# Seven block products instead of eight in the first half of a feed-forward, and a regrouped attention loop

## The chip, the cores and the metric

The kernel runs on one core of a Trainium2 chip. The metric is the device time of one execution in microseconds (us). Three executions of the kernel before took 1903.85, 1904.07 and 1905.6 us; the median is 1904.07 us. A separate profiled execution took 1902.24 us, of which 1900.5 us lie between its first and its last instruction (the span). The five engines are TensorE (PE in the profile), VectorE (DVE), ScalarE (ACT), GpSimd (POOL) and SyncE (SP); each works through a queue of its own, in order. TensorE writes its results to PSUM, eight banks of 2 KB per partition; VectorE and ScalarE move them from there to SBUF, GpSimd works in SBUF alone.

## What is computed

One transformer block on 2048 tokens of width 576, in float32:

```python
sa, ca, ga, sb, cb, gb = split(silu(c) @ w_mod, 6)
h = layernorm(x) * (1 + ca) + sa
x = x + ga * attention(h)          # 32 heads of 18, 4 segments of 512, causal inside a segment,
                                   # blended with a linear-attention memory of earlier segments
h = layernorm(x) * (1 + cb) + sb
x = x + gb * ((silu(h @ w_gate) * (h @ w_up)) @ w_down)      # 4608 wide
```

To keep float32 accuracy with TensorE's faster float32r products, each operand is split in a high and a low part, and a product is done as three: high by high, high by low, low by high.

## The kernel before, in words

**Stages.** Projections and the first attention units take the span up to about 258 us, attention goes on to about 618 us, a hand-over stretch follows, and the feed-forward runs from about 645 us to the end. It handles the tokens in two halves of 1024 (`t` 0 and 1). For each half it walks over 18 pairs `p` of 128-wide column groups of the 4608.

**One pair.** A pair has 14 steps (`k`). Each step is one block product of a seven-product (Strassen-like) scheme for gate (`z` 0) and up (`z` 1): `prod` (L1200), seven matmuls of 512 columns into bank A, B or C. Into the same steps the down product of the pair before is placed, in chunks. There are two forms of it. `plain` (L1321) is the ordinary block product: 8 chunks of 12 matmuls of 288 columns, 96 in all, each chunk added to its accumulator by VectorE (L1325). `down` (L1304) is the seven-product form: 14 chunks of 6 matmuls, 84 in all, each added by VectorE (L1309); it needs four sums of activations (`sum_a`, L1271), seven split activations (`prep_a`, L1264 and L1265) and seven split weights (`prep_d`, L1189 and L1190) where `plain` needs four of each. The function `is_plain` says which: the whole first half and the last two pairs of the second half are plain. Where chunks stand is written by hand in `CH` and `CH0`.

**Weights.** In the first half each weight tile `O` (gate or up, one pair) is loaded from the input, GpSimd makes four sums of its slots (`sum_o`, L1155), ScalarE and VectorE split each slot (`prep_w`, L1164 and L1165), and the sums are stored for the second half. The 288 input rows are 256 plus 32; the 32 left-over rows lie in a third column block of `O` and are split by `prep_r` (L1149, L1150) into the tile `R`, which is stored for the second half too. The down weights are scaled by `gb` and summed by GpSimd (`mul_d` L1178, `sum_d` L1183). Meanwhile `prep2` makes the second half's input: layernorm, transposes on TensorE (L1102), splits (L1058, L1062), sums.

**Attention.** 32 units of 4 heads (four segments, eight units each). Per unit three generators run side by side in 11 slots: score products with a running maximum on VectorE (`p1_step`, L182 and L187), score products with an exponential on ScalarE and a causal mask on GpSimd (`p2_step`, L599, L602 and L606), and the products with v (`av_step`, L619: plain float32, a 32-column weight tile per head, four heads side by side). The strings in `PAT` place everything else by hand: `V0` to `V3` are the four v steps (0 and 1 of this unit, 2 and 3 of the unit before), in four places of the unit. PSUM: two banks for the maximum's scores, two for the exponential's, one for v, two shared ones (tag `x`), one for the output projection.

**Hand-over** (L1380 to L1450). The last output projection (`wo_m`, L729), whose results VectorE adds (`wo_x`, L734), is interleaved with the first weight sums, the first `prep_r` and the first `prep_w`.

Of the kernel before, what the change touches and what calls it, by code (L numbers as in the profile page):

```python
# [15 lines left out]
P = 128  # L16
S = 2048
# [20 lines left out]
CH0 = ((0, 0, 0, 0, 1, 1, 1, 1, 1, 1, 1, 1, 0, 0), (0, 0, 0, 1, 1, 1, 1, 1, 1, 1, 1, 0, 0, 0))  # L38
RS = {(0, 5): 2, (0, 6): 4, (0, 8): 3, (0, 10): 5, (1, 9): 2, (1, 11): 3, (1, 13): 4}
# [14 lines left out]
G2 = (2, 3, 4, 5, 6, 7, 8, 9, 10, 11)  # L54
# [5 lines left out]
PAT = (["", "V2", "V3 E m D", "M0", "n M1 Q G", "c", "M2 d", "V0 g", "h A0 q M3 R S X", "T Y Z B0", "A1 P V1 z B1 f C"],  # L60
# [3 lines left out]
LNA = 1  # L64
S1B, S2B, XB, WB = 2, 2, 2, 1
# [7 lines left out]
def block(ctx: ExitStack, tc: tile.TileContext, x, wqk, wv, wo, beta, wgu, wd, c, w_mod, out):  # L73
# [76 lines left out]
    rD = [[dr.tile([96, 7, P], F32, tag=f"rD{p}_{z}", name=f"rD{p}_{z}") for z in range(2)] for p in range(NF // 2)]  # L150
# [5 lines left out]
    mcol, pmt, mrow = {}, {}, {}  # L156

    def load_stack(u, b):
        s, q = units[u]
        for e in range(2):  # L160
            v = [d[s].rearrange("f z t -> (f z) t").rearrange("(Q a e r) t -> Q e r a t", Q=8, a=2, e=2)[q, e]
                 for d in (kD, qD)]
            r = slice(54 * e, 54 * e + 54)
            nc.sync.dma_start(f32(kst[b][r]), v[0])
            nc.sync.dma_start(f32(qst[b][r, e:4:2, :]), v[1])
# [6 lines left out]
    def p1_step(u, b, i, ps, jp, jb):  # L172
# [6 lines left out]
        for h0 in range(0, 4, per):  # L179
            bank = ps.tile([P, L], F32, tag="s1", name="s1", bufs=S1B)  # L180
# [407 lines left out]
    def p2_step(u, j):  # L588
# [4 lines left out]
        pt = pp_.tile([P, 4, n], F32, tag=f"P{j}", name="Pt", bufs=1)  # L593
        Pt[u, j] = pt
        for h in range(0, 4, per):
            bank = ps.tile([P, L], F32, tag="s2", name="s2", bufs=S2B)
            for g in range(h, h + per, 2):
                w = min(per, 2)
                nc.tensor.matmul(bank[:, n * (g - h):n * (g - h + w)].rearrange("p (a b) -> p a b", a=w),  # L599
                                 lhsT=kst[u % NB][0:110, g // 2, 128 * j:128 * j + 128],  # L600
                                 rhs=qst[u % NB][0:110, g:g + w, 128 * j:L], start=True, stop=True)
            nc.scalar.activation(pt[:, h:h + per, :n], bank[:, :n * per].rearrange("p (a b) -> p a b", a=per),  # L602
                                 AF.Exp, scale=SCALE)
            if h + per < 4:
                yield
# [4 lines left out]
    def av_step(u, j):  # L610
# [3 lines left out]
        if j == 0:  # L614
            av[u] = ps.tile([P, L], F32, tag="av", name="av", bufs=1)
# [227 lines left out]
    def event(ev, u):  # L843
        n, a = ev[0], ev[1:]
        s, q = divmod(u, 8)
        if n == "V":
            j = int(a)
            av_step(u if j < 2 else u - 1, j)
# [185 lines left out]

    def y_sum(kb):
# [13 lines left out]

    def prep2(x2p):  # L1050
# [4 lines left out]
        def opr(kb, hv, o, f):  # L1055
            n = P if kb < 2 else 96
            st = x2p.tile([P, 2, 256], F32R, tag="st", name="st", bufs=4)
# [28 lines left out]
        for kb in range(3):  # L1086
            n = P if kb < 2 else 96
            for hv in range(2):
                for kh in range(2):
# [10 lines left out]
                    pt = ps.tile([P, 2, L], F32, tag="dn", name="pt", bufs=2)[:, 0].rearrange("p (a b) -> p a b", b=P)  # L1100
# [31 lines left out]
    def load_o(t, p, z):  # L1132
        O[p, z] = o = opl.tile([P, 7, 3, P], F32, tag="O", name="O", bufs=2)
        if t == 0:
            nc.sync.dma_start(o[:, 0:4], wgu[p, z])
        else:
            nc.sync.dma_start(o[:, 0:3, 0:2], wgu[p, z][:, 0:3, 0:2])
            nc.sync.dma_start(o[:, 3:7, 0:2], oD[p][z])

    def store_o(p, z):  # L1140
        nc.scalar.dma_start(oD[p][z], O[p, z][:, 3:7, 0:2])

    def prep_r(t, p, z, part=0):
        r = R[z]
        if t == 1:
            (nc.sync if p or z == 0 else nc.scalar).dma_start(f32(r[0:96]), rD[p][z])
            return
        o, c = O[p, z], slice(0, 3) if part == 0 else slice(3, 7)
        nc.scalar.copy(r[0:96, c], o[0:96, c, 2, :])  # L1149
        later.append(lambda: nc.vector.tensor_tensor(r[32:64, c], o[32:64, c, 2, :], f32(r[32:64, c]), op=ALU.subtract))  # L1150

    def sum_o(p, z, j, eng=nc.gpsimd):
        o = O[p, z]
        d, a, b, op = ((4, 3, 2, ALU.add), (5, 4, 0, ALU.subtract), (3, 0, 3, ALU.subtract), (6, 1, 5, ALU.subtract))[j]
        eng.tensor_tensor(o[:, d], o[:, a], o[:, b], op=op)  # L1155

    def store_r(p, z):
        nc.scalar.dma_start(rD[p][z], f32(R[z][0:96]))

    def prep_w(p, z, m):  # L1160
        o = O[p, z][:, SLOT[m], 0:2]
# [14 lines left out]
    def mul_d(p, f):  # L1176
        v = RW[p][:, 2 * f:2 * f + 2].rearrange("p a b -> p (a b)")
        nc.gpsimd.tensor_tensor(v, v, gbB, op=ALU.mult)  # L1178

    def sum_d(p, j):  # L1180
        r = RW[p]
        d, a, b = ((4, 1, 0), (5, 3, 4), (6, 2, 5), (1, 3, 1))[j]
        nc.gpsimd.tensor_tensor(r[:, d], r[:, a], r[:, b], op=ALU.subtract)  # L1183
# [101 lines left out]

    def load_x11(t):
# [9 lines left out]
    def down(t, p, c):  # L1296
        m, c = POS[c // 2], c % 2
        ah, al = AP[p % 2, m]
        dh, dl = DP[p % 2, m]
        pd = ps.tile([P, 2, L], F32, tag="dn", name="pd", bufs=2)  # L1300
        for i in range(2):
            tk = slice(128 * (2 * c + i), 128 * (2 * c + i) + 128)
            for k, (a, w) in enumerate(((ah, dh), (ah, dl), (al, dh))):
                nc.tensor.matmul(pd[:, i, :288], lhsT=a[:, tk], rhs=w, start=(k == 0), stop=(k == 2))  # L1304
        o = acc[m][:, 2 * c:2 * c + 2]
# [5 lines left out]
    def plain(t, p, c):  # L1311
        b, h, c = c // 4, c // 2 % 2, c % 2
        pd = ps.tile([P, 2, L], F32, tag="dn", name="pd", bufs=2)
# [9 lines left out]
        d = x11[1] if t and b and h else acc[2 + h + 2 * b]  # L1323
# [8 lines left out]
    def comb(j):  # L1332
        d, b = ((2, 1), (0, 5), (6, 1), (5, 6), (3, 5), (7, 6), (4, 7), (0, 7))[j]
        d = acc[d] if d else x11[1]
# [5 lines left out]
    with tc.manual_schedule():  # L1340
        new_stack(3, sk2)
# [4 lines left out]
        for u in range(NU + 1):  # L1346
            s, q = divmod(u, 8)
            load_unit(u + 3)
            ga = chain(*[p2_step(u, j) for j in range(4)])
            gb = p1_seq(u + 2)  # L1350
            for k in range(11):
                next(ga, None)
                next(gb, None)
                if u == 17 and k == 0:
# [30 lines left out]
        load_o(0, 0, 1)  # L1385
        load_y(0, 1)
# [13 lines left out]
        for i in range(4):  # L1400
            for h in range(2):
                for c in range(WC):
# [12 lines left out]
                    if n in WW:  # L1415
                        j = WW.index(n)
                        if j < 2:
                            prep_r(0, 0, 0, j)
# [26 lines left out]
        for t in range(2):  # L1445
            for p in range(NPR):
                last = t == 1 and p == NPR - 1
# [3 lines left out]
                if t == 0 and p == 1:  # L1451
                    p7.close()
                    x2p = pool(p6, "x2p")
                    g2 = prep2(x2p)
                if t == 0 and p == NPR - 1:
                    run(g2)
                    p6.close()
                    accq = pool(p4, "acq")
                    new_acc(accq, (1, 6, 7))
                if last:  # L1460
                    load_x11(1)
                chunk = 0
                for k in range(14):
# [6 lines left out]
                    for f in todo:  # L1470
                        f()
                    while acts:
# [14 lines left out]
                    if t:  # L1487
                        if k == 2 + swap:
                            prep_r(1, p, 1)
                        elif not last and k == 9:  # L1490
                            prep_r(1, nx, 0)
                    else:
                        if k in (3, 5):
                            prep_r(0, p, 1, k // 5)
                        elif tn == 0 and k in (9, 10):
                            prep_r(0, nx, 0, k - 9)
# [138 lines left out]
```

## Time and profile before

| | us |
|---|---|
| median of three executions | 1904.07 |
| profiled execution | 1902.24 |
| its span | 1900.5 |
| TensorE busy in the span | 1862.9 |
| VectorE busy | 1509.0 |
| ScalarE busy | 933.8 |
| GpSimd busy | 584.4 |

A busy TensorE is counted from the start of a matmul to its modelled end, and matmuls overlap: a 288-column matmul is listed with about 0.29 us, but the next one starts 0.13 us later. The cost of a matmul in a dense stretch is therefore the distance between starts. In the rows of the timeline, the columns are the start, the length, the engine, the line, the operation with its output and inputs, the shape, the count, and in brackets the idle time before it with what ended it. In the grouped rows, the columns are the busy time in us, the mean length of one in ns, and the idle time ahead of the group.

### The profile page before, as it was taken

How to read it: one execution, taken by the hardware profiler on the slowest of the kernel's cores; microseconds unless marked ns; L12 is line 12 of the kernel's file. 1: busy time of each engine (PE TensorE's matmuls, PEld its weight loads, DVE VectorE, ACT ScalarE, POOL GpSimd, SP SyncE). 2: the span in 40 equal slices, each digit the busy share in tenths (PEclk: the TensorE clock that was granted, in tenths of full speed). 3: DMA queues.
4: the chain of work that ended last, by engine and by line, in shares of the span. 5: the costliest groups of instructions: out<-in, count | busy, mean ns of one | idle time of the engine just before them, and what ended most of it. 6: DMA issues, size and time to landing. Idle time of an engine off the chain costs nothing.

```text
span 1900.5 us, 30716 instructions
## 1 busy us (share of the span) xinstructions
PE 1862.9 (98%) x10927; PEld 1559.2 (82%) x10927; DVE 1509.0 (79%) x3277; ACT 933.8 (49%) x2060; POOL 584.4 (31%) x789
## 2 busy tenths in 40 slices
PE   6999999999999899999999999999999999999999
PEld 4888866676766788888888888888888888888888
DVE  6566358878886688898898888876888888888887
ACT  1222267768767444445454454444445454454542
POOL 5212236555556555545544545400000000000000
PEclk9999999999999899999999999999999999999999
DMA  6767555446654854454454454378343233333331
GB/s 190 259 221 249 200 193 155 132 136 175 184 159 127 282 201 160 157 196 158 153 189 158 164 171 149 135 262 257 102 123 104 85 115 102 124 102 101 108 108 59
DMA packets 179424, 304.31 MB, mean 160 GB/s; under 512 B 26152, under 2 KB 107688, under 8 KB 177352
## 3 DMA queue, kind: packets, MB, share of 16 engines
q1 hardware_dynamic: 150696, 245.29, 40.9%
q10 hardware_dynamic: 28576, 57.07, 8.6%
q8 instruction: 86, 1.41, 0.3%
q14 instruction: 66, 0.54, 0.1%
HBM read 187.98 MB, written 113.77 MB: 159 GB/s over the span
## 4 chain that ended last, share of the span: by engine, by line
PE 90%; DVE 3%; DMA 2%; ACT 2%; POOL 1%; issue 1%; SPq 0%; ACTq 0%; DVEq 0%; POOLq 0%
PE A L1200 23%; PE pd L1321 13%; PE C L1200 12%; PE pd L1304 9%; PE B L1200 6%; PE pp L99 6%; PE s L599 4%; PE av L619 4%; PE s L182 4%; PE pv L99 2%; PE pw L729 2%; PE pn L800 1%; PE px L640 1%; ACT Pt L602 1%; PE pm L448 1%
## 5 line engine op out<-in xcount | busy, mean ns | idle before, releaser
L1200 PE MATMUL A<-y,wh 128*128 128x512 f32 x1152 | 404.5, 392 | 1.7 <-ACT B L1246 1.1
L187 DVE CUSTOM_DVE_ANT_0 junk<-s,tri 128x256 bf16<-128x256 f32 (+3 forms) x512 | 228.4, 486 | 68.4 <-PE s L182 60.9
L1165 DVE TENSOR_TENSOR wl<-O,wh 128x256 fp32r<-128x256 f32 x504 | 264.1, 529 | 3.3 <-ACT wh L1164 2.8
L1200 PEld LDWEIGHTS A<-y,wh 128*128 128x128 f32 x1152 | 216.7, 188 | 42.6 <-ACT B L1246 1.7
L1200 PE MATMUL A<-y,wl 128*128 128x512 f32 x576 | 224.8, 390 | 0.0
L602 ACT ACTIVATE Pt<-s 128x512 f32<-128x512 f32 (+1 forms) x352 | 187.9, 559 | 70.2 <-PE s L599 64.4
L1155 POOL TENSOR_TENSOR O<-O 128x384 f32<-128x384 f32 x140 | 158.1, 1142 | 174.3 <-DMA O<-in_wgu_dram 78.8
L1200 PE MATMUL C<-y,wh 128*128 128x512 f32 x576 | 203.6, 394 | 3.8 <-DMA y<-yD 2.5
L1309 DVE TENSOR_TENSOR acc<-acc,pd 128x576 f32<-128x576 f32 x216 | 162.2, 751 | 54.8 <-PE pd L1304 50.6
L1164 ACT CAST wh<-O 128x256 fp32r<-128x256 f32 x504 | 196.9, 405 | 0.8 <-issue 0.7
L1321 PE MATMUL pd<-dh,ah 128*128 128x288 f32 x640 | 189.8, 297 | 0.3 <-DVE acc L1325 0.3
L1321 PE MATMUL pd<-dh,al 128*128 128x288 f32 x640 | 188.2, 294 | 0.0
L1321 PE MATMUL pd<-dl,ah 128*128 128x288 f32 x640 | 188.1, 294 | 0.0
L1325 DVE TENSOR_TENSOR acc<-acc,pd 128x576 f32<-128x576 f32 x156 | 116.7, 749 | 81.8 <-PE pd L1321 81.7
L1264 ACT CAST ah<-sg 128x512 fp32r<-128x512 f32 x192 | 119.3, 621 | 86.1 <-DVE sg L1224 80.4
L599 PE MATMUL s<-qs,ks 110*128 110x512 f32 (+2 forms) x384 | 150.1, 407 | 2.9 <-ACT Pt L602 2.4
L182 PE MATMUL s<-ks,qs 108*128 108x256 f32 (+3 forms) x512 | 140.4, 327 | 1.9 <-DVE mx L187 1.8
L1265 DVE TENSOR_TENSOR al<-sg,ah 128x512 fp32r<-128x512 f32 x192 | 135.6, 707 | 7.1 <-ACT ah L1264 6.8
L1304 PE MATMUL pd<-dh,ah 128*128 128x288 f32 x448 | 132.9, 297 | 0.0
L1304 PE MATMUL pd<-dl,ah 128*128 128x288 f32 x448 | 131.9, 294 | 0.0
L1304 PE MATMUL pd<-dh,al 128*128 128x288 f32 x448 | 131.2, 293 | 0.0
L1200 PEld LDWEIGHTS C<-y,wh 128*128 128x128 f32 x576 | 108.1, 188 | 24.1 <-DMA y<-yD 2.9
(364 smaller groups left out, 4410.9 us busy)
## 6 DMA issues: line engine op xcount, KB each, us to landing
O<-in_wgu_dram SPq DMA_DIRECT2D x36, 768.0 KB
oD<-O ACTq DMA_DIRECT2D x36, 512.0 KB
O<-oD SPq DMA_DIRECT2D x36, 512.0 KB
ks<-kD SPq DMA_DIRECT2D x64, 216.0 KB
qs<-qD SPq DMA_DIRECT2D x64, 216.0 KB
O<-in_wgu_dram SPq DMA_DIRECT2D x36, 384.0 KB
rD<-wr ACTq DMA_DIRECT2D x36, 336.0 KB
wr<-rD SPq DMA_DIRECT2D x35, 336.0 KB
```

Of the source, the lines that this page charges most:

```text
L99: nc.tensor.matmul(ps, lhsT=a, rhs=b, start=(k == 0), stop=(k == 13))
L182: nc.tensor.matmul(bank[:, n * (h - h0):n * (h - h0) + n], lhsT=qst[b][0:108, h, 128 * i:128 * i + 128], rhs=kst[b][0:108, h // 2, 0:n], s ...
L187: nc.vector.tensor_tensor_reduce(junk[:, :n], bank[:, n * (h - h0):n * (h - h0) + n], tri[:, L - n:], 1.0, -3e38, op0=ALU.add, op1=ALU.max ...
L599: nc.tensor.matmul(bank[:, n * (g - h):n * (g - h + w)].rearrange("p (a b) -> p a b", a=w), lhsT=kst[u % NB][0:110, g // 2, 128 * j:128 * ...
L602: nc.scalar.activation(pt[:, h:h + per, :n], bank[:, :n * per].rearrange("p (a b) -> p a b", a=per), AF.Exp, scale=SCALE)
L1155: eng.tensor_tensor(o[:, d], o[:, a], o[:, b], op=op)
L1164: nc.scalar.copy(wh, o)
L1165: later.append(lambda: nc.vector.tensor_tensor(wl, o, f32(wh), op=ALU.subtract))
L1200: nc.tensor.matmul(bank, lhsT=a, rhs=b, start=(first and n == 0), stop=(n == 6), skip_group_check=not first)
L1304: nc.tensor.matmul(pd[:, i, :288], lhsT=a[:, tk], rhs=w, start=(k == 0), stop=(k == 2))
L1309: nc.vector.tensor_tensor(o, o, pd[:, :, :288], op=ALU.add)
L1321: nc.tensor.matmul(pd[:, i, :288], lhsT=a[:, tk], rhs=w, start=(k == 0), stop=(k == 5))
```

## The change

In the first half, pairs 0 to 15 now use the seven-product form of the down product, as the second half does; only the last two pairs of each half stay plain. The first half's accumulators are combined in its last pair (`comb`, eight additions), as was done in the second half alone.

- **Chunks on ScalarE.** In the first half, for pairs 1 to 15, the odd chunks (seven of fourteen) do not go through VectorE: ScalarE first copies the accumulator into the PSUM bank (`preload`), TensorE adds the products to it, and ScalarE copies the sum back. The two PSUM buffers of the down product become two tags of one buffer each, `dn0` for even and `dn1` for odd chunks.
- **Left-over rows.** `prep_r` is gone. The left-over rows are an input of their own (`wgr`), summed by GpSimd, copied by ScalarE and subtracted by GpSimd in the attention stage (`stage_r`: nine batches, one every two units, 4 sums, 4 copies and 4 subtractions each), stored, and loaded into `R` by three DMAs per weight tile in both halves. `O` shrinks from three column blocks to two.
- **GpSimd in pieces.** `sum_o` works in pieces of 128 elements per partition, eight per weight tile where there were four of 384; `mul_d` and `sum_d` in pieces of 144 (before 576 and 288). `mul_d` and `sum_d` move to steps 3 to 5, the first tile's `sum_o` to steps 5 to 8.
- **Second half's preparation.** `prep2` may go on in 13 steps of a pair instead of 10; its transposes use `dn0` in steps 6, 7 and 12 alone, and it has three split buffers instead of four.
- **Attention.** The four v steps of a unit are done in one burst at the start of the next unit, between the first score product and its exponential, and their bank comes from the shared tag `x`. The maximum's scores get a third bank. The stacked q and k are loaded in pieces of 96 and 12 and of 48 and 6 partitions instead of 54, as an event of the pattern. `PAT` is rewritten.

```diff
-S1B, S2B, XB, WB = 2, 2, 2, 1
+S1B, S2B, XB, WB = 3, 2, 2, 1
...
+    def stage_r():
...
+            for j, (d, x_, y_, op) in enumerate(SUMS):
+                at(max(0, g + RL[1 + j]), lambda ...: nc.gpsimd.tensor_tensor(o[:, d], o[:, x_], o[:, y_], op=op))
+            for j in range(4):
+                c = slice(32 * j, 32 * j + 32)
+                at(g + RL[5 + j], lambda ...: nc.scalar.copy(h[:, :, c], o[:, :, c]))
+                at(g + RL[9 + j], lambda ...: nc.gpsimd.tensor_tensor(o[:, :, c], o[:, :, c], f32(h[:, :, c]), op=ALU.subtract))
...
+    def preload(t, p, c):
+        if t == 0 and p > 0 and c in AS:
+            PRE[c] = pd = new_dn("pd", c)
+            nc.scalar.copy(pd[:, :, :288], chunk_of(c))
...
     def down(t, p, c):
+        o = chunk_of(c)
+        pd = PRE.pop(c, None)
+        add = pd is None
+        if add:
+            pd = new_dn("pd", c)
...
+        if not add:
+            outs.append(lambda: nc.scalar.copy(o, pd[:, :, :288]))
+            return
...
     def is_plain(t, p):
-        return t == 0 or p >= NPR - 2
+        return p >= NPR - 2
...
             for k in range(11):
                 next(ga, None)
+                if k == BK and u:
+                    for j in range(4):
+                        av_step(u - 1, j)
+                next(ga, None)
                 next(gb, None)
...
+                    while outs:
+                        outs.pop(0)()
+                    if prev is not None and not is_plain(*prev):
+                        for c in range(chunk, chunk + CH[k] + CH[(k + 1) % 14]):
+                            if not PRE:
+                                preload(*prev, c)
```

More of the change, by code (lines that the diff above doesn't have):

```diff
@@ L1177, in mul_d @@
         v = RW[p][:, 2 * f:2 * f + 2].rearrange("p a b -> p (a b)")
-        nc.gpsimd.tensor_tensor(v, v, gbB, op=ALU.mult)
+        for c in range(0, 576, 144):
+            nc.gpsimd.tensor_tensor(v[:, c:c + 144], v[:, c:c + 144], gbB[:, c:c + 144], op=ALU.mult)
     def sum_d(p, j):
@@ L1303, in down @@
             for k, (a, w) in enumerate(((ah, dh), (ah, dl), (al, dh))):
-                nc.tensor.matmul(pd[:, i, :288], lhsT=a[:, tk], rhs=w, start=(k == 0), stop=(k == 2))
-        o = acc[m][:, 2 * c:2 * c + 2]
+                nc.tensor.matmul(pd[:, i, :288], lhsT=a[:, tk], rhs=w, start=(add and k == 0), stop=(k == 2),
+                                 skip_group_check=not add)
+        if not add:
+            outs.append(lambda: nc.scalar.copy(o, pd[:, :, :288]))
+            return
         if p == 0 and m not in (2, 3, 4):
@@ L1322, in plain @@
                     k += 1
[L1323 removed]
+        d = x11[t] if b and h else acc[2 + h + 2 * b]
         o = d[:, 2 * c:2 * c + 2]
@@ L1486, in block @@
                         load_o(tn, nx, 1)
[L1487 to L1496, printed above, removed]
-                        elif tn and k == 8:
-                            prep_r(1, 0, 0)
+                    if k == 2 + swap:
+                        load_r(p, 1)
+                    elif not last and k == 9:
+                        load_r(nx, 0)
+                    if t == 0:
                         if k == 1 and p:
```

171 lines of the change are left out of this document (101 added, 70 removed), and 6 rows, old and new, of the table PAT.

## The prediction

> **What bounds the kernel now.** I read the page's totals first, then the busy times by stretch, then the chain of work that ended last.
>
> ```profile
> span 1900.5 us, 30716 instructions
> PE 1862.9 (98%) x10927; PEld 1559.2 (82%) x10927; DVE 1509.0 (79%) x3277; ACT 933.8 (49%) x2060; POOL 584.4 (31%) x789
> ```
>
> ```profile
> 300.00:600.00 300.00, 298.03 (x2209) 206.31 (x2208) 246.85 (x1013) 222.81 (x460) 166.31 (x330) 1.00 0.53 152
> 618.00:645.00 27.00, 21.56 (x137) 20.43 (x137) 17.16 (x32) 9.80 (x21) 13.55 (x14) 0.87 0.67 240
> 645.00:705.15 60.15, 55.30 (x272) 46.70 (x273) 50.43 (x76) 31.23 (x70) 33.34 (x30) 0.97 0.68 235
> 705.15:1307.92 602.77, 602.24 (x3347) 533.69 (x3347) 505.92 (x770) 283.45 (x660) 260.91 (x236) 1.00 0.54 177
> ...
> 953.81:1130.91 177.10, 177.10 (x988) 157.15 (x987) 153.53 (x227) 85.64 (x200) 86.89 (x78) 1.00 0.51 167
> 1324.67:1660.61 335.94, 335.94 (x1822) 295.34 (x1821) 291.58 (x542) 164.09 (x380) 0.00 (x0) 1.00 0.34 107
> ```
>
> After the stretch and its length stand the busy times of PE, PE's weight loads, DVE, ACT and POOL, then the granted clock. TensorE idles for 2 us of 300 in attention, for 0.5 us of 603 in the first half of the feed-forward, and for 10.3 us of 87 in the hand-over between them, where its clock also dropped to 0.87. So elsewhere a matmul less is time less, as long as VectorE (87% busy in the first half: 153.53 of 177.10) keeps up.
>
> ```profile
> 701.95 1.59 PE pd L1321 x12
> 703.54 1.61 PE C L1200 x7
> 705.15 3.17 PE A L1200 x14
> ...
> 1307.92 3.18 PE A L1200 x14
> ```
>
> These are pieces of the chain: start, length, matmuls. The last two rows stand at the same place of two pairs, 17 pairs apart: (1307.92 - 705.15) / 17 = 35.46 us a pair in the first half. The 335.94 us of the last stretch above are ten pairs of the second half, 33.59 us each. Twelve 288-column matmuls take 1.59 us, 0.1325 each, and twelve is what `plain` has more than `down` (96 against 84): 33.59 + 1.59 = 35.18; the other 0.28 us are the transposes of `prep2`.
>
> **Step 1: the products, -25.4 us.** Sixteen pairs lose 12 matmuls each: 16 x 1.59 = 25.4 us. Nothing is added on TensorE in this stage. This holds if the other engines fit in a pair of 33.59 + 0.28 = 33.9 us.
>
> **Step 2: VectorE in the new first half.**
>
> ```profile
> 1009.06 0.74 DVE L1325 TENSOR_TENSOR acc<-acc,pd 128x576 f32<-128x576 f32 x1
> 1009.73 0.57 DVE L1165 TENSOR_TENSOR wl<-O,wh 128x256 fp32r<-128x256 f32 x1
> ```
>
> ```profile
> L1165 DVE TENSOR_TENSOR wl<-O,wh 128x256 fp32r<-128x256 f32 x70 | 45.5, 659 | 0.0
> ...
> L1062 DVE TENSOR_TENSOR st<-ha,st 128x256 fp32r<-128x256 f32 x12 | 8.5, 705 | 0.0
> ...
> L1190 DVE TENSOR_TENSOR dl<-dr__13341,dh 128x288 fp32r<-128x288 f32 x4 | 3.6, 909 | 0.1
> ```
>
> ```profile
> L1165 DVE TENSOR_TENSOR wl<-O,wh 128x256 fp32r<-128x256 f32 x140 | 58.4, 417 | 0.0
> ...
> L1190 DVE TENSOR_TENSOR dl<-dr__18649,dh 128x288 fp32r<-128x288 f32 x7 | 3.2, 451 | 0.0
> ```
>
> The second half already does all that a new pair needs, without GpSimd: 291.58 / 10 = 29.2 us. A chunk's addition holds VectorE for 1009.73 - 1009.06 = 0.67 us; seven go to ScalarE, -4.7. The `prep2` splits add 8.5 / 5 = 1.7. That is 26.2 us. On top comes waiting for GpSimd: the same split takes 659 ns in the first half (first fence, five pairs) and 417 ns in the second, the down-weight split 909 and 451. Fourteen of the one and four of the other wait 3.4 + 1.8 = 5.2 us a pair; seven of the other make it 3.4 + 3.2 = 6.6, and the four new sums I put at 0.7 more.
>
> ```profile
> 1002.90 1.02 POOL L1155 TENSOR_TENSOR O<-O 128x384 f32<-128x384 f32 x1 [5.87 <-DMA O<-in_wgu_dram]
> 1003.88 1.43 POOL L1178 TENSOR_TENSOR dr__12568<-dr__12568,gbB 128x576 f32<-128x576 f32 x1
> ```
>
> ```profile
> 1003.91 1.68 DVE L1062 TENSOR_TENSOR st<-ha,st 128x256 fp32r<-128x256 f32 x1
> ```
>
> The last row shows what the waiting is: a split that started as GpSimd's 1.43 us product ran ended 0.28 us after it. The two GpSimd rows give 2.14 ns per element and 0.20 us per instruction, so a piece of 128 takes an estimated 0.47 us and one of 144 0.51. A pair has 16 of each: 15.7 us, about what whole ones took (86.89 / 5 = 17.4 with `prep2`). The blocker is shorter, but there are more of them. So the waiting lies between 3.6 (half of 7.3, as the piece is less than half as long) and 7.3; I take 5.5. VectorE then needs 31.7 us of 33.9, at most 33.5. It fits, narrowly; local lateness I price at 0.2 us a pair, 3 us. In pair 1 the seven odd chunks still go to VectorE, + 4.7, which makes 36.4 and costs once 2.5, say 3 us. **Sum +6 us**, bounds 0 and +20 (1 us a pair, and pair 1 at 4).
>
> **Step 3: ScalarE.**
>
> ```profile
> L631 ACT COPY avs<-av 128x512 f32<-128x512 f32 x26 | 15.2, 585 | 0.4
> ...
> L809 ACT COPY nm<-pn 128x380 f32<-128x380 f32 (+1 forms) x24 | 10.6, 442 | 9.4 <-PE pn L800 9.4
> ```
>
> Copies between SBUF and PSUM of 576 elements aren't in the trace; from 512 elements in 585 ns, 0.65 us each (between the mean of 442 ns for smaller ones and VectorE's 0.74), the way into PSUM taken like the way out. Fourteen make 9.2 us on the 85.64 / 5 = 17.1 of a first-half pair; six more casts at no more than 0.65 make 30.2 of 33.9. What matters is the order: bank `dn1` goes copy back, copy in, products. At steps 4 and 12 an even chunk and a step's seven matmuls lie between, 0.79 + 1.6 = 2.4 us against two copies, 1.3 us, so 1 us of lateness is covered; at the other chunks a whole step more. I price it at nothing; without the cover each late microsecond would count twice a pair, 32 us in all.
>
> **Step 4: attention, -8 us.** TensorE pays for changing between float32r products and the v products.
>
> ```profile
> 404.27 0.40 PE L599 MATMUL s<-qs,ks 110*128 110x512 f32 x1
> 404.50 0.39 PE L182 MATMUL s<-ks,qs 108*128 108x512 f32 x1
> 404.82 0.64 PE L619 MATMUL av<-Pt,vq 128*32 128x256 f32 x8
> 405.39 0.50 PE L599 MATMUL s<-qs,ks 110*128 110x512 f32 x1
> 405.73 0.39 PE L182 MATMUL s<-ks,qs 108*128 108x512 f32 x1
> ```
>
> ```profile
> 613.79 1.01 PE L619 MATMUL av<-Pt,vq 128*32 128x256 f32 x16 [0.38 <-POOL Pt L606]
> 614.73 0.40 PE L729 MATMUL pw<-woh,oh 128*128 128x288 f32 x1
> ```
>
> Between two score products of 512 columns lie 0.23 us (404.27 to 404.50); ahead of the v step it is 0.32, behind it 0.34: 0.09 in and 0.11 out. In the instruction order of the two programs the entries into v products go from 126 to 32, and the returns from them to float32r products from 71 to 31: 94 x 0.09 + 40 x 0.11 = 12.9 us. The v steps themselves get no shorter: the two adjacent ones at 613.79 (256 and 128 columns) take 0.94 us together, as 0.57 (404.82 to 405.39) and 0.36 apart. The transposes that stood right behind a v step now change modes on their own; nothing up to 0.11 each for some 25, so gross gain 10 to 13; I take 12. Against it: in a burst of 2.7 us TensorE feeds neither VectorE (82% busy) nor ScalarE (74%). VectorE has three banks to drain, three elevenths of its 9.4 us a unit, so it idles little; ScalarE stands about 2 of 11.4 us and needs 8.5. I price these waits at 4 us over 32 units (bounds 0 and 20). `stage_r` adds 72 GpSimd operations of 0.5 to 0.7 us, about 41 us in the first 18 units, beside 55% busy; they fill the burst and cost nothing unless a mask comes late. More DMA issues on SP precede use by a whole unit. **Sum -8**, bounds -13 and +10.
>
> By the Trainium skill (TensorEngine Tiling (Array Packing), Key Properties), changing the tiling mode drains TensorE; a v step is 128 x 32 tiles, a score product the full array. The 0.09 and 0.11 us agree; the page gives no price.
>
> **Step 5: hand-over, -6.6 us.**
>
> ```profile
> 631.62 0.62 ACT L1149 CAST wr<-O 96x512 fp32r<-96x512 f32 x1 [5.97 <-POOL O L1155]
> ```
>
> ```profile
> 634.43 0.61 PE L729 MATMUL pw<-woh,oh 128*128 128x288 f32 x1 [4.14 <-DVE xr L734]
> 634.84 0.44 PE L729 MATMUL pw<-wol,oh 128*128 128x288 f32 x1
> ...
> 639.64 0.38 PE L729 MATMUL pw<-wol,oh 128*128 128x288 f32 x1
> ```
>
> `prep_r` waits for all four GpSimd sums, VectorE waits behind it, and TensorE stands for 4.14 us behind VectorE, then runs 0.24 us a matmul instead of 0.1325 until 639.64: some 20 matmuls and the first one's longer start, 2.3 us. Without `prep_r` the first split that needs a sum is three places later and needs two sums, not four. What is late next are the loads of y and O, issued behind the same work, so they move along. The gain is 4.14 + 2.3 = 6.4, with 0.2 for smaller loads 6.6; bounds 0 (the loads are the limit anyway) and -10.
>
> By the Trainium skill (TensorE: Matmul & The Clock Gate, Part 1), an idle window of about 3.4 us halves the clock; 0.24 against 0.1325 agrees roughly, and a wait cut below that would save the slow stretch too.
>
> **The sum.** -25.4 + 6 - 8 - 6.6 = -34.0. From the profiled execution's 1902.24 us (span plus 1.7) that is 1868.2; the median stands 1.8 above it, so **1870 us**.
>
> **The rivals.**
> - *Attention waits* (15%): late masks or full score banks cost 20 us instead of 4, as GpSimd goes from 55% to about 75% in the first units: 1904.07 - 25.4 + 6 + 8 - 6.6 = 1886. For it: PE's few waits there are for masks (0.38 above). Against: a mask has over 2 us of burst ahead of its use.
> - *The first half becomes bound by ScalarE's chain or by VectorE* (15%): a pair stays at about 35 us, so the change doesn't do what it says: -25.4 + 20 - 8 - 6.6 = -20, 1884.
> - *Slower: the pieces lock VectorE out* (8%). If every piece of GpSimd's blocks a VectorE operation for its whole length, as single rows show, waiting is up to 15.7 us a pair, VectorE needs up to 42 us, and the pair grows. The point at which all gains are gone: 33.9 + 40 / 16 = 36.4 us, waiting of 10.2 us, 65% of GpSimd's time, against 30% shown (5.2 of 17.4). At 80%, 12.6 us, a pair takes 38.8: +78 - 40 = 1942. The Trainium skill (SBUF — State Buffer, Who interferes with whom) has such a rule: a VectorE instruction with two SBUF inputs and a GpSimd one that reads SBUF exclude each other for the whole instruction. The split of 1.68 us agrees; that only 30% of the time is lost speaks against the whole price.
> - *Better* (7%): no waits, full hand-over gain: 1904.07 - 25.4 - 13 - 10 = 1856.
>
> **How the numbers follow.** The forecast (1860 to 1880) has 55%. The range 1854 to 1890 takes in both dearer rivals that stay faster. About 0.2% (4 us) can be told from no change: faster 0.9 (all cases but the slower one, less 0.02 for their far ends), same 0.02, slower 0.08.
>
> **What would show it.** A pair of 33.6 to 34.2 us in the first half with TensorE's idle time under 2%; split (wl) means near 600 ns; 32 bursts of v products with the row behind each at 0.34; no 4 us wait at the output projection. I am wrong if TensorE waits for `pd` or `acc` in the first half, or for `Pt` in each unit.

## The result, and the profile after

The changed kernel takes **1872.39 us** (median of four, 1870.86 to 1875.27), the kernel before beside it 1903.96 us (1903.31 to 1905.6): a ratio of 0.9838 [0.9827, 0.985], or -31.6 us, where -34.0 was predicted. The profiled execution took 1873.81 us, 1.4 above the median, as the one before lay 1.7 below its own; so the two profiles differ by 28.4 us.

The totals of the page of the changed kernel, then busy times by stretch (columns as in the prediction: PE, weight loads, DVE, ACT, POOL, clock, DMA share, GB/s):

```profile
span 1872.1 us, 31670 instructions
...
PE 1829.1 (98%) x10735; PEld 1546.2 (83%) x10735; DVE 1492.9 (80%) x3364; ACT 1075.6 (57%) x2330; POOL 681.3 (36%) x1173
```

```profile
300.00:600.00 300.00, 293.04 (x2273) 221.78 (x2271) 245.00 (x1028) 238.78 (x505) 202.30 (x395) 1.00 0.68 183
607.70:630.80 23.10, 21.69 (x170) 20.58 (x158) 16.40 (x34) 9.67 (x20) 14.25 (x18) 1.00 0.91 310
...
687.99:1234.67 546.68, 546.22 (x2973) 477.83 (x2973) 483.12 (x810) 401.99 (x864) 314.03 (x507) 1.00 0.49 158
1234.67:1279.11 44.44, 38.84 (x195) 33.50 (x195) 20.25 (x40) 13.82 (x33) 0.00 (x0) 0.92 0.82 272
687.99:1166.12 478.13, 477.67 (x2597) 417.15 (x2597) 426.66 (x719) 363.96 (x781) 293.89 (x475) 1.00 0.49 157
1234.67:1260.00 25.33, 21.26 (x110) 17.77 (x109) 12.23 (x23) 7.88 (x18) 0.00 (x0) 1.00 1.02 345
```

The last v product ends at 607.7 us here and at about 614.5 before, the second feed-forward product starts at 630.8 (before 645.0), and 687.99, 1234.67 and 1279.11 are the same places as 705.15, 1272.71 and 1307.92 before. So the 28.4 us divide like this:

| stretch | before | after | difference | predicted |
|---|---|---|---|---|
| to the last v product | 614.5 | 607.7 | -6.8 | -8 |
| hand-over, to the second feed-forward product | 30.5 | 23.1 | -7.4 | -6.6 |
| to the mark in the first half | 60.2 | 57.2 | -3.0 | |
| sixteen pairs from it | 567.6 | 546.7 | -20.9 | -19.4 with the row above |
| the pair at the switch of halves | 35.2 | 44.4 | **+9.2** | nothing |
| the rest | 592.6 | 593.0 | +0.4 | 0 |

Fourteen undisturbed first-half pairs take 478.13 / 14 = 34.15 us each (before 35.46), and TensorE idles for 0.46 us in all of them. Two things stand out: the first half did better than priced, and one pair, the first of the second half, lost 9.2 us that no step of the prediction has. The chain of that pair (start, length, what), a row of SP's queue and one of TensorE's say why:

```profile
1234.67 3.17 PE A L1234 x14
...
1241.19 11.33 DMA y<-yD
...
1252.54 8.94 DMA wr<-rD
...
1262.32 2.88 PE pd L1373 x12
...
1279.11 3.18 PE A L1234 x14
```

```profile
1248.86 3.98 SPq L1178 DMA_DIRECT2D wr<-rD  x3
```

```profile
1261.53 0.80 PE L1234 MATMUL A<-y,wr 128*128 128x512 f32 x1 [4.02 <-DMA wr<-rD]
```

The left-over rows of the second weight tile (`load_r`) are issued by SP behind the last loads of y (issued up to 1242.77), at 1248.86, and land 12.6 us later, while the DMA engines are full (share 1.02, 345 GB/s up to 1260). TensorE waits 4.02 us for them, and then runs twelve 288-column matmuls in 2.88 us instead of 1.59 and seven products of 512 columns in 2.73 instead of 1.6. Two waits for loads of y, 1.3 us in all, stand before that. In the kernel before, its timeline shows, ScalarE issued this load, eight us into the pair:

```profile
1280.69 0.31 ACTq L1146 DMA_DIRECT2D wr<-rD  x1
```

### The profile page after: what moved, and what is told of

Same layout as the page of the kernel before. It is cut to its first block, busy times and chain, and to the rows that moved or that the text cites. A ratio compares the mean times of both kernels' runs of the same rounds, so it can differ in the third digit from the quotient of the medians.

```text
span 1872.1 us, 31670 instructions
## 1 busy us (share of the span) xinstructions
PE 1829.1 (98%) x10735; PEld 1546.2 (83%) x10735; DVE 1492.9 (80%) x3364; ACT 1075.6 (57%) x2330; POOL 681.3 (36%) x1173
## 4 chain that ended last, share of the span: by engine, by line
PE 86%; DVE 4%; DMA 4%; ACT 3%; issue 2%; POOL 1%; SPq 0%; POOLq 0%; ACTq 0%; DVEq 0%
PE A L1234 24%; PE pd L1353 19%; PE C L1234 12%; PE B L1234 6%; PE pp L105 5%; PE s L188 3%; PE av L627 3%; PE s L603 3%; PE pd L1373 2%; PE pw L737 2%; PE pv L105 2%; ACT Pt L610 1%; DMA y<-yD 1%; DVE junk L193 1%; PE pn L808 1%
## 5 line engine op out<-in xcount | busy, mean ns | idle before, releaser
L1361 DVE TENSOR_TENSOR acc<-acc,pd 128x576 f32<-128x576 f32 x327 | 245.3, 751 | 79.9 <-PE pd L1353 73.8
L1353 PE MATMUL pd<-dh,ah 128*128 128x288 f32 x896 | 268.3, 299 | 1.1 <-DVE acc L1359 0.7
L1353 PE MATMUL pd<-dl,ah 128*128 128x288 f32 x896 | 264.2, 295 | 0.0
L1353 PE MATMUL pd<-dh,al 128*128 128x288 f32 x896 | 262.9, 293 | 0.0
L1353 PEld LDWEIGHTS pd<-dh,ah 128*128 128x128 f32 x896 | 168.4, 188 | 21.1 <-ACT pd L1329 4.0
L1299 DVE TENSOR_TENSOR al<-sg,ah 128x512 fp32r<-128x512 f32 x240 | 177.0, 738 | 8.5 <-ACT ah L1298 8.4
L1353 PEld LDWEIGHTS pd<-dl,ah 128*128 128x128 f32 x896 | 169.8, 189 | 16.0
L1189 POOL TENSOR_TENSOR O<-O 128x128 f32<-128x128 f32 x280 | 155.0, 586 | 69.2 <-DVE wl L1196 19.7
L1353 PEld LDWEIGHTS pd<-dh,al 128*128 128x128 f32 x896 | 169.4, 189 | 0.0
L1234 PEld LDWEIGHTS A<-y,wl 128*128 128x128 f32 x576 | 108.6, 188 | 14.8
```

Of the source, the lines that this page charges most:

```text
L1189: eng.tensor_tensor(o[:, d, i, s_], o[:, a, i, s_], o[:, b, i, s_], op=op)
L1234: nc.tensor.matmul(bank, lhsT=a, rhs=b, start=(first and n == 0), stop=(n == 6), skip_group_check=not first)
L1299: later.append(lambda: nc.vector.tensor_tensor(al, src, f32(ah), op=ALU.subtract))
L1361: nc.vector.tensor_tensor(o, o, pd[:, :, :288], op=ALU.add)
```

## The experiments

Differences are to the changed kernel's 1872.39 us, unless another kernel is named; ratios are to the kernel before.

### The late rows at the switch of halves

```diff
-    def load_r(p, z):
+    def load_r(p, z, eng=nc.sync):
...
+            eng.dma_start(f32(R[z][32 * i:32 * i + 32]), rD[b][i % 2][32 * g:32 * g + 32])
...
-                        load_r(p, 1)
+                        load_r(p, 1, nc.scalar if swap else nc.sync)
```

> The changed kernel, with one thing other: the three loads of the left-over rows of the second weight tile, in the first pair of the second half, are issued by ScalarE's queue instead of SyncE's, behind no loads of y. Theory 1 (the pair at the half switch took 44.4 us instead of 35.2 because TensorE waits 4.0 us for these loads, which stand behind y's in one queue, and runs slowly after it): 6 to 9 us faster than the changed kernel, 1863 to 1866, and no wait for wr<-rD. Rival (the y loads fill the DMA engines, and TensorE would wait for one of them anyway): 0 to 2 us faster.

Measured: **1866.25 us**, ratio 0.9804 [0.9789, 0.9819], -6.1. This is the best version of the study, ahead of both kernels. In its chain, as above:

```profile
1231.04 3.17 PE A L1234 x14
...
1237.98 11.81 DMA y<-yD
...
1269.30 2.72 PE A L1234 x12
```

The pair takes 38.26 us, 6.2 less than in the changed kernel; the wait for `wr` is gone, as the first theory has it. Of the other 3 us, 1.6 are TensorE's waits for loads of y, which take 11.8 us from issue to landing, and 0.9 is a wait for an addition on VectorE. They were not taken further.

### The chunks on ScalarE

```diff
-AS = (1, 3, 5, 7, 9, 11, 13)
+AS = ()
```

> The changed kernel with all fourteen chunks of the first half added by VectorE, none on ScalarE. Theory 1 (VectorE is close to its limit: 30.5 us of 34.15 a pair, and seven additions of 0.67 us make it 35.2): a pair of 35.2 us or more, at least 16 us slower than the changed kernel, 1888 or more. Rival (VectorE still has room, as in the second half, where it does all fourteen): at most 4 us slower.

Measured: 1889.22 us, +16.8, ratio 0.9925 [0.9908, 0.9941]. With all chunks on VectorE, TensorE waits for its additions (us in all, times, longest):

```profile
PE pd L1353 <- DVE acc L1361: 8.1, 12, 1.0
```

Its transposes wait for additions 3.5 us more, its matmuls 2.5 us for ScalarE's `ah`. Nine pairs take (1166.13 - 847.78) / 9 = 35.4 us each in this kernel's chain, where 35.2 or more were expected. So the step with ScalarE is needed: without it two thirds of the 25.4 us of the fewer products are lost to waiting.

### The first half with plain products

```diff
     def is_plain(t, p):
-        return p >= NPR - 2
+        return t == 0 or p >= NPR - 2
...
```

`comb` stays in the second half alone, and one accumulator more is loaded there at the switch. The work is that of a plain first half, but `sum_d` writes over the slot of one of the four plain down weights before it is split: that weight has other values here, and as many operations.

> The changed kernel with the first half's down products in the plain form again (96 matmuls a pair, 8 additions on VectorE, no combination at the end); all else of the change stays. Theory 1 (the products are worth their 16 x 12 x 0.1325 us): 24 to 26 us slower than the changed kernel, 1896 to 1898. Rival (part of the gain is lost to waits on VectorE and ScalarE): 10 to 18 us slower.

Measured: 1893.36 us, +21.0, ratio 0.9946 [0.9931, 0.9961]. It lies between the two, nearer to the first: the first half's products and what comes with them carry about what the table gives the first half (-23.9), and the rest of the change is worth some 10 us without them.

### GpSimd's sums in whole instructions

All three kinds whole (`sum_o`, `mul_d`, `sum_d`):

```diff
...
-        for c in range(0, 576, 144):
-            nc.gpsimd.tensor_tensor(v[:, c:c + 144], v[:, c:c + 144], gbB[:, c:c + 144], op=ALU.mult)
+        nc.gpsimd.tensor_tensor(v, v, gbB, op=ALU.mult)
...
```

> The changed kernel with GpSimd's sums and products of the weights in whole instructions (256, 576 and 288 elements) instead of pieces of 128 and 144. Theory 1 (VectorE waits longer for a longer instruction, 7.3 instead of 4.2 us a pair, 33.6 in all, and just fits): splits of 0.60 us or more instead of 0.55, 0 to 6 us slower. Rival 1 (the pieces are what lets VectorE keep up): a pair above 35 us, over 15 us slower. Rival 2 (the number of pieces is what costs): faster by 2 us or more.

Measured: 1898.82 us, +26.4, ratio 0.9975 [0.9966, 0.9984]. VectorE was busy for 435.12 of 482.04 us in fourteen pairs (90%, 89% in the changed kernel), so its mean load is not what bounds. The timeline of VectorE where a pair's `mul_d` and `sum_d` run, with whole instructions:

```profile
843.47 1.66 DVE L1092 TENSOR_TENSOR st<-ha,st 128x256 fp32r<-128x256 f32 x1
845.05 1.66 DVE L1196 TENSOR_TENSOR wl<-O,wh 128x256 fp32r<-128x256 f32 x1
846.63 1.30 DVE L1302 TENSOR_TENSOR sg<-sg 128x512 f32<-128x512 f32 x1
```

and at the same place of the changed kernel, in pieces:

```profile
833.02 0.71 DVE L1092 TENSOR_TENSOR st<-ha,st 128x256 fp32r<-128x256 f32 x1
833.66 0.72 DVE L1196 TENSOR_TENSOR wl<-O,wh 128x256 fp32r<-128x256 f32 x1
834.29 0.98 DVE L1305 TENSOR_TENSOR sg<-sg 128x512 f32<-128x512 f32 x1
```

GpSimd beside the first of these two:

```profile
842.88 3.55 POOL L1209 TENSOR_TENSOR dr__11385<-dr__11385,gbB 128x576 f32<-128x576 f32 x2 [3.81 <-DVE cu L1254]
```

Its two products take 1.77 us each and end at about 844.65 and 846.43; the two splits that start beside them end 0.5 and 0.3 us later. Three VectorE instructions in a row lose 2.2 us, and the additions behind them come late. Two more runs part the down weights from the gate and up weights:

> The changed kernel with only the weight sums of sum_o as whole GpSimd instructions (8 of 256 elements a pair), the sums and products of the down weights still in pieces. All three whole cost 26.4 us. Theory 1: the cost comes at steps 3 to 6 of a pair, where the whole down instructions (two of 576, four of 288 elements, 8 us in a row) hold VectorE's additions of the even chunks back; sum_o alone, which lies at steps 5 to 8, 10 and 11, costs 2 to 10 us: 1874 to 1882 us. Rival: the cost goes by the elements that GpSimd works on in long instructions wherever they lie, and the two halves of it (2048 and 2304 elements a pair) cost about the same: +10 to +14 us here, 1882 to 1887 us.

> The changed kernel with only the down weights' products and sums (mul_d, sum_d) as whole GpSimd instructions, sum_o still in pieces: the other half of the same question. Theory 1: these carry the loss, +15 to +25 us, 1887 to 1897 us, with TensorE's waits for an addition on VectorE back at steps 3 to 6 of a pair. Rival: the loss goes by elements, +12 to +15 us, 1884 to 1887 us. Third: the two only hurt together, since a backlog of one has to meet the other; then each alone costs under 6 us, and the sum of both runs' losses is far under 26 us.

Measured: `sum_o` whole 1871.66 us, -0.7, ratio 0.9827 [0.981, 0.9844], not to be told from the changed kernel; the down weights whole **1895.32 us**, +22.9, ratio 0.9952 [0.9937, 0.9966] (the kernel before took 1905.61 us beside these two). The first theory holds, and its 2 to 10 us for `sum_o` were too much. TensorE's waits in the first half of the latter kernel:

```profile
PE pd L1350 <- DVE acc L1358: 7.2, 8, 3.0
PE pd L1350 <- ACT pd L1326: 3.6, 8, 0.5
```

Its weight loads wait 14.3 us for the same additions. What costs is not GpSimd's time: from 690 to 1170 us it is busy for 237.35 us in this kernel and for 293.89 in the changed one. What is left is the length of an instruction, 1.77 us for a whole product of the down weights and 0.90 for a whole sum in `sum_o`, and its place, where additions are due; the two runs differ in both and do not part them.

### The attention loop

The old loop, banks and stack pieces in the changed kernel (`stage_r` stays):

```diff
-S1B, S2B, XB, WB = 3, 2, 2, 1
+S1B, S2B, XB, WB = 2, 2, 2, 1
...
-                if k == BK and u:
-                    for j in range(4):
-                        av_step(u - 1, j)
...
```

> The changed kernel with the attention loop of before (v products in four steps, their own bank, two banks for the maximum's scores, the old pattern and stack pieces); the left-over rows' stage and the feed-forward stay as changed. Theory 1 (mode changes of TensorE, 12 us gross, 4 lost to waits): 5 to 9 us slower than the changed kernel, 1877 to 1881. Rival (the burst's gain is lost to waits): within 2 us.

Measured: 1885.48 us, +13.1, ratio 0.9913 [0.9898, 0.9927]: the new loop is worth more than the prediction gave it. Its last v product ends at 617.8 us, 3.3 later than before the change, so that about 3 us seem to be what `stage_r` costs the old loop. The old loop with the new pieces was not run, so the 13.1 us are the loop's and the pieces' together. The burst split in two by a score product:

```diff
                         av_step(u - 1, j)
+                        if j == 1:
+                            next(gb, None)
...
-                next(gb, None)
+                if not (k == BK and u):
+                    next(gb, None)
```

> The changed kernel with the burst of v products cut in two by one score product (of the maximum), which then comes earlier by half a burst. Theory 1 (each entry costs 0.09 and each return 0.11 us): 31 more of each, 6 us slower. Rival (the burst starves VectorE and ScalarE, and a score product inside it feeds them): no slower, or faster.

Measured: 1881.46 us, +9.1, ratio 0.9884 [0.9865, 0.9903]: more than the two mode changes a unit. The rows tell where from. One unit of the kernel before, of the changed kernel and of the split one:

```profile
400.09 1.07 PE L619 MATMUL av<-Pt,vq 128*32 128x512 f32 x8
401.09 0.50 PE L599 MATMUL s<-qs,ks 110*128 110x512 f32 x1
...
402.92 0.85 PE L619 MATMUL av<-Pt,vq 128*32 128x384 f32 x8
403.70 0.50 PE L599 MATMUL s<-qs,ks 110*128 110x512 f32 x1
...
```

```profile
402.72 0.45 PE L603 MATMUL s<-qs,ks 110*128 110x512 f32 x1
403.09 2.36 PE L627 MATMUL av<-Pt,vq 128*32 128x512 f32 x32
405.39 0.50 PE L188 MATMUL s<-ks,qs 108*128 108x512 f32 x1
```

```profile
395.04 1.71 PE L627 MATMUL av<-Pt,vq 128*32 128x512 f32 x16
396.68 0.50 PE L188 MATMUL s<-ks,qs 108*128 108x512 f32 x1
397.11 0.86 PE L627 MATMUL av<-Pt,vq 128*32 128x256 f32 x16
397.90 0.50 PE L603 MATMUL s<-qs,ks 110*128 110x512 f32 x1
```

From start to the next start, the four steps apart take 1.00 + 0.78 + 0.57 + 0.36 = 2.71 us (the last two as in the prediction), in two groups 1.64 + 0.79 = 2.43, in one burst 2.30. Each join saves 0.13 to 0.14 us in the v products themselves. Going in is dearer than the 0.09 us that were expected: the score product ahead of the burst takes 0.37 us (402.72 to 403.09), the one inside the split burst 0.43 (396.68 to 397.11), where two score products lie 0.23 apart. So a split costs one join (0.13), 0.20 going in and 0.11 coming out. 29 of the 32 units have a score product to put in: 29 x 0.44 = 12.8 us, against 9.1 measured. TensorE waits 1.1 us less in the split kernel, from 200 us to the last v product; the rest of the difference was not followed.

### The stack's pieces

The 54-partition pieces back in the changed kernel:

```diff
-        for r0, r1 in ((0, 96), (96, 108)):
-            nc.sync.dma_start(f32(kst[b][r0:r1]), k[r0:r1])
...
+            r = slice(54 * e, 54 * e + 54)
+            nc.sync.dma_start(f32(kst[b][r]), v[0])
```

> The changed kernel with the stacked q and k loaded in pieces of 54 partitions again. Theory 1 (the loads precede their use by a unit and nothing waits for them): within 2 us. Rival (pieces of 54 land later and the first score products of a unit wait): over 4 us slower.

Measured: 1888.98 us, +16.6, ratio 0.9931 [0.9904, 0.9958] (the profiled execution took 1896.34). TensorE's waits in attention, then the chain at one of them:

```profile
PE s L604 <- DMA qs<-mr: 9.0, 6, 2.8
```

```profile
306.75 6.16 DMA qs<-mr
```

The row of maxima (8 KB) is issued at 306.18, 2.5 us behind the first and 1.3 behind the last of four pieces of 216 KB, and takes 6.16 us. These waits are less than half of the loss; besides, from 300 to 600 us the granted clock is 0.97 here and 1.00 in the changed kernel. The old loop bears the same pieces, with 1.7 us of waits for the rows. Two runs asked whether its place in the queue is the cause. The rows on ScalarE's queue:

```diff
-            nc.sync.dma_start(f32(qst[b][108 + a:109 + a])...
+            nc.scalar.dma_start(f32(qst[b][108 + a:109 + a])...
```

> The changed kernel with the 54-partition stack pieces of the kernel before (as in the run with the old stack pieces, 1888.98 us, +16.6 on the changed kernel), and the small rows of maxima (qs<-mr, 8 KB) issued on ScalarE's queue, not on SP's behind the stack loads. Theory 1: with the old pieces TensorE waits because these rows stand in SP's queue behind the 216 KB pieces; on a queue of their own they land in time, the waits for qs<-mr (9.0 us in 6 waits) fall below 2 us, and most of the 16.6 us comes back: 1872 to 1880 us. Rival: the pieces hold the DMA engines themselves, whatever queue the rows are in, or the stack pieces land late for their own score products: the rows' waits stay over 5 us or others take their place, 1884 to 1895 us. Cost of the edit that both allow: two more issues on ScalarE in each of 32 units, off the path as long as the exponentials are not what ends last.

Measured: 1915.95 us, ratio 1.0055 [1.0038, 1.0071], some 25 more than with the old pieces alone (27 by the medians, 24 by the ratios). The run doesn't answer the question, since its edit costs more than the thing it tests, on the engine whose issues were taken for free. ScalarE's timeline, and TensorE's waits for it:

```profile
409.01 1.15 ACTq L177 DMA_DIRECT2D qs<-mr  x2
```

```profile
PE s L604 <- ACT Pt L611: 30.7, 39, 3.5
PE s L604 <- DMA qs<-mr: 3.9, 5, 1.4
```

Two issues hold ScalarE for 1.15 us a unit, 37 us in 32 units, in front of the exponentials that free TensorE's banks; the waits for these were 4.8 us with the old pieces alone. The rows' own waits fell, from 9.0 to 3.9 us. The other way is to leave the rows on SP and put them ahead of the pieces:

```diff
-PAT = (["E", "", "U m D", "M0", "n M1 Q G", ...
+PAT = (["E", "", "m D", "M0", "n U M1 Q G", ...
```

> The changed kernel with the old 54-partition stack pieces (alone 1888.98 us, +16.6), and the loads of the next stack moved in each unit from slot 0 or 2 to behind the small rows of maxima (slot 2 or 4), so that on SP's queue the rows go ahead of the four pieces; nothing is added on any engine. In the run with the old pieces a row issued at 306.18 us, 1 to 2.5 us behind the four pieces, landed after 6.16 us, and TensorE's next score product waited for it. Theory 1: the rows are late because they stand behind the pieces; ahead of them they land in time, the waits for qs<-mr (9.0 us in 6 waits) fall below 2 us and most of the loss comes back: 1872 to 1879 us. Rival: the pieces are slow wherever they stand; issued 2 to 4 us later they are late for the score products of their own unit (waits for qs<-qD and ks<-kD) or for the rows of the next: 1884 to 1900 us.

Measured: **1925.9 us**, ratio 1.0119 [1.0102, 1.0136], 37 more than with the old pieces alone. TensorE's waits in attention, and the chain at one of them:

```profile
PE s L189 <- DMA ks<-kD: 16.8, 16, 2.6
PE s L189 <- DMA qs<-qD: 14.8, 21, 1.1
```

```profile
405.28 7.39 DMA qs<-qD
```

No wait for the rows is left; the pieces are late instead, 31.6 us in all, and the last of the four lands 7.4 us after its issue. The rival is right: the pieces are slow wherever they stand, and what comes behind them is late. In the changed kernel the chain of attention has one such piece, of 192 KB, and it is quicker:

```profile
496.59 4.76 DMA qs<-qD
```

While the late piece of the other run is under way (404.0 to 412.7 us), the DMA engines are busy for a share of 0.76, at 202 GB/s; here (495.4 to 501.4 us) it is 1.02, at 254 GB/s. So with the old pieces a quarter of the DMA engines' time is idle while TensorE waits for a load. The Trainium skill (DMA: Bandwidth & Descriptors, Why a DMA increments its semaphore by 16 and not by 1) says that a transfer runs on the largest number of engines up to 16 that divides the slowest dimension on both of its sides; by that, an estimate, 54 partitions would take 9 engines, and 96 or 48 would take 16. The shares and the two landing times agree with that; no row here shows which engines a transfer used, so the reason for the slowness stays the page's.

### The hand-over alone

The kernel before, with the second part of its first `prep_r` seven places later:

```diff
-                        if j < 2:
-                            prep_r(0, 0, 0, j)
+                        if j in (0, 3):
+                            prep_r(0, 0, 0, j // 3)
```

> The kernel before, with the second part of the first left-over split in the hand-over seven places later (where the fourth weight split stands). Theory 1 (this split, waiting for four GpSimd sums, made the 4.14 us wait at the output projection and 2.3 us of slow matmuls after it): 5 to 7 us faster than the kernel before, 1897 to 1899, and no wait above 1 us at the output projection. Rival (the loads of y and of the weights end the hand-over whatever it does): within 2 us of it.

Measured: 1898.56 us, -4.5 against the kernel before beside it (1903.06), ratio 0.998 [0.9967, 0.9992], so between 1.5 and 6.3 us. TensorE's waits from the last v product to the mark in the first half:

```profile
PE C L1200 <- DVE cu L1223: 2.7, 1, 2.7
PE C L1200 <- DMA y<-yD: 2.7, 1, 2.7
PE pw L729 <- DVE xr L734: 1.6, 2, 1.3
```

The 4.14 us wait is down to 1.3, where none above 1 was expected. Of the two behind it, the one for y was there before (2.5 us) and is in the changed kernel too (2.8), and the one for `cu` was 1.3 us, so that some of the gain is given back there.

## Why the prediction was right, and where it was not

**Step 1, the products: right.** 84 matmuls a pair run in 34.15 us, inside the 33.6 to 34.2 that were named, and TensorE doesn't idle. With plain products 21.0 of the 31.6 us are gone.

**Step 2, VectorE: right in kind, too dear by 4.5 us.** In the fourteen pairs' window VectorE needs 426.66 / 14 = 30.5 us a pair, not 31.7. By shape, over the same fourteen pairs of the changed kernel:

```profile
L1196 DVE TENSOR_TENSOR wl<-O,wh 128x256 fp32r<-128x256 f32 x196 | 106.7, 550 | 0.6
```

The split takes 550 ns (before 659), so of the 242 ns above the second half's 417 it lost nearly half. The pieces are longer than estimated: eight products in 5.60 us, 0.70 each instead of 0.51.

```profile
832.05 5.60 POOL L1210 TENSOR_TENSOR dr__11497<-dr__11497,gbB 128x144 f32<-128x144 f32 x8 [3.75 <-DVE cu L1257]
```

The estimate for 128 elements, 0.47, fits in attention; in the first half the same shape takes longer. That VectorE's work beside it is the reason is not shown. Both rows are of the changed kernel, the first from 255 to 608 us, the second from the fourteen pairs:

```profile
L1049 POOL TENSOR_TENSOR yh<-yh 128x128 f32<-128x128 f32 x33 | 14.9, 461 | 0.9
L1189 POOL TENSOR_TENSOR O<-O 128x128 f32<-128x128 f32 x224 | 125.2, 592 | 54.3 <-DVE dl L1224 16.9 <-DVE wl L1196 16.6 <-DMA O<-in_wgu_dram 15.5
```

GpSimd is then busy for 293.89 / 14 = 21.0 us a pair, more than before, and yet VectorE's split waits less. The count of GpSimd's time, from which the step worked, was the wrong measure; what the runs with whole sums point to is the one long instruction that is met where results are due (+22.9 us at one place, nothing with shorter ones at another). Pair 1 took 34.7 us (653.28 to 687.99 in the chain), not 36.4. The slower rival, pieces that lock VectorE out, did not come. The Trainium skill (SBUF — State Buffer, Who interferes with whom) says that a VectorE instruction with two SBUF inputs and a GpSimd one that reads SBUF contend for a shared port, an exclusive lock; the timeline of the whole sums agrees, where two splits of 0.7 us took 1.66 beside products of 1.77.

**Step 3, ScalarE: right.** Its two copies by shape take 644 and 641 ns for an estimated 650; it is busy for 26.0 us a pair, less than the 30.2 that were counted, and TensorE's weight loads wait for the copy in for 4.0 us in fourteen pairs.

```profile
L1329 ACT COPY pd<-acc 128x576 f32<-128x576 f32 x98 | 63.1, 644 | 2.2
L1356 ACT COPY acc<-pd 128x576 f32<-128x576 f32 x97 | 62.2, 641 | 28.3 <-PE pd L1353 28.3
```

```profile
PEld pd L1353 <- ACT pd L1329: 4.0, 14, 0.4
```

**Step 4, attention: the sum nearly right (-6.8 for -8), three of its parts wrong, so the sum is partly luck.** "The v steps themselves get no shorter" fails: an undisturbed unit's four take 2.30 us instead of 2.71. The row that was to show it hid the join, since its second step waited for its mask; a row of TensorE's weight loads in the kernel before says so:

```profile
614.37 0.16 PEld L619 LDWEIGHTS av<-Pt,vq 128*32 128x32 f32 x8 [0.43 <-POOL Pt L606]
```

The second step starts 0.59 us behind the first there, and 0.46 behind it in the split burst, where nothing holds it. The second part that fails is the 12 us for the mode changes. From 200 us to the last v product, each matmul counted to the start of the next one and the waits left out, the v products take 76.5 us, against 87.0 with the old loop in the same kernel, and all other matmuls 319.3, against 323.7: about 4 us where 12 were priced, and twelve transposes that now come after this mark are in that. One reason is the way into the burst, which costs 0.14 us instead of 0.09. Two of the 32 bursts, besides, ran 3.9 us each, between 258 and 300 us, where the granted clock was 0.92. So 10.5 + 4.4 us, less 4.7 that TensorE waits longer, make 10.2; the last v product comes forward by 10.1 beside the old loop (617.8 to 607.7). The third part is "More DMA issues on SP precede use by a whole unit", priced at nothing, which misses what the pieces do: with the old pieces the burst is worth nothing (1888.98 us against 1885.48 with the old loop), and with the new ones 13.1. Against this gain stand TensorE's idle time, 7.0 us of 300 instead of 2.0, near the 4 us of waits that were named, and the cost of `stage_r`, which seems to be about 3 us.

**Step 5, hand-over: right.** -7.4 for -6.6; the clock in the stretch is 1.00 instead of 0.87, and moving `prep_r` alone brings 4.5 (1.5 to 6.3). The loads of y did move along: the one wait for them, behind this stretch, was 2.5 us and is 2.8.

**What was missing: the switch of halves, +9.2 us.** The prediction counted the 72 operations of `stage_r` and not the three loads for each weight tile that the change puts on SP's queue in both halves, 216 where there were 35. TensorE waits for them once, where they stand behind the loads of y. The first run shows it: 6.1 of the 9.2 us come back when they go on another queue. The sum came out near since this loss and the first half's better price (4.5 us) stand against each other; so much of it was luck.

## What to carry to other kernels

When an operation of an engine is replaced by a load, price the load at the worst moment of its queue, not the usual one, and see what stands ahead of it; in these runs rows of 8 KB and of 112 KB landed 6.2 and 12.6 us after their issue behind larger loads. When GpSimd and VectorE share work, look for the longest single GpSimd instruction beside a due VectorE one, not at either one's busy time: cutting the down weights into pieces was worth 22.9 us, cutting the others nothing. Edits that look apart may only pay together: the burst brought nothing without the new pieces, and the fewer products a third of their gain without ScalarE's chunks.

## What the runs showed of the hardware beside this

- Groups of v products in 32-column tiles run 0.13 to 0.14 us faster per join than apart (2.71, 2.43 and 2.30 us for the same 32 matmuls). The change from full products to them costs 0.09 us ahead of a single step, 0.14 ahead of the burst and 0.20 in the split one, the change back 0.11.
- A GpSimd piece of 144 elements takes 0.70 us in the first half, where the line through the whole ones gave 0.51; one of 128 takes 592 ns there and 461 ns in the attention stage.
- Two issues of 8 KB transfers hold ScalarE for 1.15 us (at 409.01 in the run with the rows on its queue).
- After the 4.02 us wait at 1261.53 TensorE started its next twelve 288-column matmuls 0.24 us apart; at 1267.77 they were back at 0.13.
